# Sliding-window attention and gated FFN on one core: the first w_gate group in halves of x, a hundred small matmuls on zeros, two weight loads in two pieces

## The chip, the core and the metric

The kernel runs on one core of one Trainium2 chip. The core has five engines that run side by side and wait for each other through semaphores: TensorE (PE) does matmuls, with its weight loads shown apart (PEld); VectorE (DVE), ScalarE (ACT) and GpSimd (POOL) work on elements; SyncE (SP) starts transfers. POOL starts most of the loads here. The metric is the device time of one execution in microseconds, the median of several runs. Before the change it is 298.24 us, from 298.19 to 298.33 in three runs.

## What is computed

Attention over 8 batches of 8 heads, 576 positions of depth 64, where each position sees itself and the 63 before it. Its output, laid out as 4608 tokens of 512, goes through a gated feed-forward block.

```python
scores = scale * np.matmul(q, k.transpose(0, 1, 3, 2))
rel = pos[:, None] - pos[None, :]
scores = np.where((rel >= 0) & (rel < 64), scores, -1000000000.0)
attn = softmax(scores)                       # over the last axis
x = np.matmul(attn, v)                       # as [4608, 512]
gate = np.maximum(x @ w_gate, 0.0)           # w_gate, w_val: [512, 1536]
out = gate * (x @ w_val) @ w_out             # w_out: [1536, 512]
```

## The kernel before

**Tokens and tiles.** Attention works in units of 192 positions. The feed-forward block takes tokens in tiles: tile 0 has 384 (units 0 and 1), tile 1 has 192 (unit 2), tile 2 has 448, all later ones 512. From tile 2 on, products are formed by seven instead of eight block products (fast_hidden, L740; SevenOut, L966); tiles 0 and 1 use plain matmuls. The operands are 16 bits wide, the sums 32.

**Weights.** Model depth 512 is cut into four chunks c = 0..3 of 128, the 1536 hidden units into twelve blocks f = 0..11 of 128. w_gate and w_val are each loaded in thirds (f = 0..3, 4..7, 8..11), each third as two loads (w_load, L155 to L163): half a = 0 has c = 0 and 1, half a = 1 has c = 2 and 3. POOL issues them, one after another, among loads of q, k, v and w_out. In the built program each of POOL's loads also waits until the load eight before it has landed. w_out comes in thirds of one load each (L162).

**The start.** q and k of batch 0 are loaded; DVE and ACT turn them into 16 bits (L193) and DVE transposes them (L200). Meanwhile PE writes the mask's bias into all eight banks (bias_mm, L244), and matmuls on zeros (keep_hot, L241; heat, L238) stand at some places between real ones. Scores (L277), exp on ACT (L311), then P·V (u_pv, L348) for units 0 and 1, each in two halves hh of four heads. The norm of a half (reciprocal L362, then multiplication on DVE, L369, or on ACT, L381) and a transpose on DVE (u_turn, L391) give a half of x: half hh = 0 is depth c = 0 and 1, half hh = 1 is c = 2 and 3. P·V of unit 0 lies in banks 0 and 1, that of unit 1 in banks 2 and 3, and the first hidden blocks go to the same four banks, so each bank must have been read by its norm first. The order on DVE is unit 0 half 0, unit 0 half 1, unit 1 half 0, unit 1 half 1.

**first_hidden (L646).** f = 0..3 of tile 0, in four blocks n of 384 columns, each in one bank. Block 0 is f = 0 and 1 on unit 0; block 1 is f = 2 on both units; block 2 is f = 3 on both units; block 3 is f = 0 and 1 on unit 1. A list STEPS says in which order (block, chunks c, units, whether it ends) PE goes through them, first for w_gate (relu on ACT, L677), then for w_val (the product with the relu on DVE, the gate, L683 and L686). Blocks 1 and 2 of w_gate are done in matmuls of 384 columns (L667), all others in matmuls of 192 (L672).

**hidden (L590).** f = 4..11 of tile 0 and all f of tile 1 (L634), relu L605, gate L609. The argument halves = {(first f, 0 for w_gate or 1 for w_val): count} says how many blocks at the front of a group of four are run with c = 0, 1 for all of them before c = 2, 3. SPLIT lists the blocks whose 384 columns are done as two matmuls of 192.

**output (L1168, out_mm L1138).** Tile 0 with the first 128 tokens of tile 1, in four subs of 128 tokens and three cuts of f (0..3, 4..7, 8..11). For OUT_SPLIT <= f < 11 a 512-wide matmul is done as two of 256.

**The order.** One program order is written by hand and by a planner. A Weaver keeps a clock: matmuls advance it by their estimated time, and work of the other engines is put in at a planned time (W.at) or when a landing time given with w_load has come (w_need). So an engine's order follows from estimates, and the chip then runs each engine's queue in that order. Work of unit 2 (its scores, exps, masks L318, P·V and v copies on POOL, L216) is put among the hidden blocks of tile 0 in this way.

Of the kernel before, what the change touches and what calls it, by code (L numbers as in the profile page):

```python
# [10 lines left out]
FP32 = mybir.dt.float32  # L11
FP16 = mybir.dt.float16
# [35 lines left out]
def kernel(  # L48
# [10 lines left out]
    nc = tc.nc  # L59
# [7 lines left out]
    NC = DM // 128  # L67
    NF = DF // 128
    G = 4
    scale = 1.0 / float(D) ** 0.5  # L70
    TT = 2 * U
# [17 lines left out]
    singles = [psum.tile([128, 512], FP32, name=f"bank{i}") for i in range(8)]  # L89
# [9 lines left out]
    us = persist.tile([128, 4, 2, 128 * HF], FP16)  # L99
# [33 lines left out]
    def v_fixed(i, eng):  # L133

        eng.memset(v16s[i][:, :, :, D:VW].bitcast(FP32), ONE_ONE)
        eng.memset(v16s[i][0:64, 0].bitcast(FP32), 0.0)
# [6 lines left out]
    units = {}  # L143
# [3 lines left out]
    def xt_tile(t):  # L147
        if t not in xts:
            xts[t] = x_sb.tile([128, NC, WT], FP16, name="xt")
        return xts[t]  # L150
# [1 line left out]

    w_done = {}

    def w_load(wt, src, f0, f1, landed):  # L155

        if wt is not wo:
            ns = slice(128 * f0, 128 * f1)
            for a in range(2):
                nc.gpsimd.dma_start(wt[:, 2 * a:2 * a + 2, ns], src.rearrange("(a p e) n -> a p e n", a=2, e=2)[a, :, :, ns])  # L160
        if wt is wo:
            nc.gpsimd.dma_start(wo[:, f0:f1], src.rearrange("(c p) n -> p c n", p=128)[:, f0:f1])  # L162
        w_done.update(((wt.name, f, a), landed - 1.3 * (1 - a)) for f in range(f0, f1) for a in range(2))  # L163

    def w_need(wt, f, a=1):
        while (wt.name, f, a) not in w_done:
            W.pop()
        W.advance(w_done[wt.name, f, a])
# [7 lines left out]
    def qk_load(b, name, hh):  # L176

        tile_ = nat[b, name, hh] = nats[:, 2 * "kq".index(name) + hh]
        src = (q if name == "q" else k)[b, G * hh:G * hh + G]
        nc.gpsimd.dma_start(tile_, src.rearrange("h (i j) d -> (h i) (j d)", i=32))  # L180
# [21 lines left out]
    def v_load(u, parts=None):  # L202

        b, uu = divmod(u, UB)
        for g, lo, hi in parts or (((1, 0, 128), (3, 0, 128)), ((5, 0, 128),), ((7, 0, 128), (NG - 1, 64, 128)))[uu]:
            nc.gpsimd.dma_start(v16s[b % 2][lo:hi, g, :, 0:64],  # L206
                                v[b, :, 64 * g - 64 + lo:64 * g - 64 + hi].rearrange("h p d -> p h d"))
# [27 lines left out]
    def heat(n, to, start=True):  # L235

        for _ in range(n):
            nc.tensor.matmul(to, zero[:, 0:128], zero[:, 0:to.shape[1]], start=start, stop=start, skip_group_check=not start)  # L238
# [9 lines left out]
    def one_bank():  # L248
        taken["one"] += 1
        to = singles[(taken["one"] - 1) % 4]  # L250
        while id(to) in unread:
            W.pop()
        return to
# [9 lines left out]
    def st_tiles(u):  # L263
        d = units.setdefault(u, {})
        if u == 0:
            d["st"] = [one_bank() for _ in range(G)]
        else:
            halves = [two_banks() for _ in range(2)]
            d["st"] = halves[0] + halves[1]
        part_written(d["st"])  # L270
        d["p"] = [None] * G
# [23 lines left out]
    def u_st(u, hhs=(0, 1)):  # L295
        d = units.setdefault(u, {})
        if "st" not in d:
            st_tiles(u)
        run_rows([[st_block(d["st"][g][:, U * hh + 64 * w:U * hh + 64 * w + 64], g, hh, UB * u + w, "biased" in d)
                   for hh in hhs for w in range(UB)] for g in range(G)])  # L300
        return 0.29 * len(hhs)
# [117 lines left out]
    def part_written(banks):  # L419
        written.update((id(to), 0) for to in banks)  # L420
# [225 lines left out]
    def first_hidden():  # L646

        g_sb, done = gs[0] = g_sb_p.tile([128, NF, WT], FP16, name="g_sb"), {}
        xt = xt_tile(0)
        r2s = [f_sb.tile([128, 2, WT], FP32, name="pr", bufs=4) for _ in range(2)]  # L650
        r_sbs = [r2s[n // 2][:, n % 2, 0:TT] for n in range(4)]
        blocks = (((0, 0), (1, 0)), ((2, 0), (2, 1)), ((3, 0), (3, 1)), ((0, 1), (1, 1)))
        parts = lambda tile: tile.rearrange("p (w n) -> p w n", w=2)
        STEPS = (
            ((0, (0, 1), (0, 1), False), (0, (2, 3), (0, 1), True), (1, (0, 1), (0, 1), False), (2, (0, 1), (0, 1), False), (1, (2, 3), (0, 1), True), (2, (2, 3), (0, 1), True), (3, (0, 1, 2, 3), (0, 1), True)),
            ((0, (0, 1), (0, 1), False), (2, (0, 1), (0, 1), False), (0, (2, 3), (0, 1), True), (2, (2, 3), (0, 1), True), (3, (0, 1, 2, 3), (0, 1), True), (1, (0, 1, 2, 3), (0, 1), True)),
        )

        def products(h, i, n, cs, us=(0, 1), more=False):
            wt = (wg, wv)[i]  # L660
            block = blocks[n]
            W.advance(W.clock)
            w_need(wt, block[-1][0], cs[-1] // 2)
            whole = i == 0 and n in (1, 2)
            for c in cs if whole else ():
                f = block[0][0]
                nc.tensor.matmul(h[:, 0:TT], wt[:, c, f * 128:f * 128 + 128], xt[:, c, 0:TT],  # L667
                                 start=(c == 0), stop=(c == NC - 1), skip_group_check=True)
            for m in () if whole else us:
                f, u = block[m]  # L670
                for c in cs:
                    nc.tensor.matmul(h[:, U * m:U * m + U], wt[:, c, f * 128:f * 128 + 128], xt[:, c, U * u:U * u + U],  # L672
                                     start=(c == 0 and m == us[0] and not more), stop=(c == NC - 1), skip_group_check=True)
            W.clock += len(us) * len(cs) * (U + 7) / 2400.0

        def relu(n, h):
            nc.scalar.activation(r_sbs[n], h[:, 0:TT], ACT.Relu)  # L677

        def gate(n, h):
            (f, u), (f1, u1) = blocks[n]  # L680
            if f == f1:
                to = g_sb[:, f:f + 1, 0:TT]
                nc.vector.tensor_tensor(to, r_sbs[n].rearrange("p (w n) -> p w n", w=1), h[:, 0:TT].rearrange("p (w n) -> p w n", w=1), MUL)  # L683
                done[f] = TT
            else:
                nc.vector.tensor_tensor(g_sb[:, f:f + 2, U * u:U * u + U], parts(r_sbs[n]), parts(h[:, 0:TT]), MUL)  # L686
                done.update({f: U * u + U, f1: U * u + U})

        for i, then in enumerate((relu, gate)):
            hs = {}  # L690
            for n, cs, us, ends in STEPS[i]:
                more = n in hs
                if not more:
                    hs[n] = one_bank()
                    part_written([hs[n]])
                products(hs[n], i, n, cs, us, more and 0 not in us)
                if ends:
                    W.at(W.clock, lambda n=n, h=hs[n], then=then: then(n, h))
# [186 lines left out]
    wts = persist.tile([128, 4, HF, QN], FP16)  # L885
# [296 lines left out]

    LAST = len(widths) - 1
    BY_ACT = ()
    SPLIT, OUT_SPLIT = [(i, f) for i in range(2) for f in range(4, NF)], 7
    HALVED = [(4, 0, 'P5')] + [(4, 1, name) for name in ('P1', 'P2', 'P3', 'P4')]
    FAST_OUT = (LAST - 5, LAST - 4, LAST - 3, LAST - 2, LAST - 1, LAST)
    O_SUMS = {2: [(24.0, 2, (1, 1)), (26.0, 0, (0, 1))], 3: [(8.0, 3, (1, 0)), (34.0, 1, 2), (34.1, 3, 0)]}
# [8 lines left out]
    with tc.manual_schedule():  # L1197
        G3, V3, O3 = ([(wt, src, f0, f0 + 4) for f0 in (0, 4, 8)]
                      for wt, src in ((wg, moe_w_gate), (wv, moe_w_val), (wo, moe_w_out)))
# [2 lines left out]
            first_load(name)  # L1202
        for name in "kq":
            qk_load(0, name, 1)
        warm = consts.tile([128, 2], FP32)
        nc.vector.memset(warm, 0.0)
        nc.scalar.activation(warm[:, 1:2], warm[:, 0:1], ACT.Exp)
        for i in range(2):
            v_fixed(i, nc.vector)
        zero32 = wts.rearrange("p a f n -> p (a f n)").bitcast(FP32)[:, 0:384]  # L1210
        nc.vector.memset(zero32, 0.0)
        zero = zero32.bitcast(FP16)
        st_tiles(0)
        bands()
        v_load(0, ((1, 0, 128), (3, 0, 64)))
        v_load(1, ((3, 64, 128), (5, 0, 128)))
        w_load(*G3[0], 15.2)
        w_load(*V3[0], 17.7)
        k_zeros()
        band_bias()  # L1220
# [25 lines left out]
        u_turn(0, (0,))  # L1246
        for hh in range(2):
            u_pv(1, (hh,), True)
        heat(1, units[1]["st"][3])
        for hh in range(2):  # L1250
            u_recip(1, (hh,))
        u_norm_act(1, 1)
# [4 lines left out]
        w_load(*G3[1], 20.3)  # L1257
        w_load(*V3[1], 22.8)
        v_load(2)
        w_load(*G3[2], 27.0)  # L1260
        w_load(*V3[2], 29.6)
        W.at(22.0, lambda: u_st(2))
        plan_exps(22.0, 2)
        plan_values(26.4, 2)
# [96 lines left out]

        W.advance(15.3)
        first_hidden()
        hidden(0, ((0, TT),), 4, NF, 4, split=SPLIT, halves={(8, 0): 4, (8, 1): 3})
        hidden(1, ((0, U),), each=4, banks=[0, 1, 4, 5, 2, 3, 0, 1, 2, 3, 0, 1])
        taken["one"] += 2
        output(0, (0, 1, 2, 3), (0, 4, 8, NF))
# [71 lines left out]
```

## Time and profile before

| what | value |
|---|---|
| median of 3 runs | 298.24 us (298.19 to 298.33) |
| the profiled execution | 298.17 us |
| its span, first to last instruction | 296.5 us |
| PE busy | 286.9 us, 97% of the span, 4659 matmuls |
| DVE / ACT / POOL busy | 255.4 / 203.5 / 190.2 us |
| DMA queue of POOL's loads | 49376 packets, 20.26 MB, 57.9% of 16 engines' span |

The profile lists instructions with engine, source line, result and operands. A matmul's duration is its whole passage; how fast matmuls follow each other is read from their starts. "idle before" and "<-" tell how long an engine had nothing to run and what ended that. The chain of work that ended last is followed back from the last instruction, at each step to what released it. The view of transfers gives the time from a load's issue to its landing; issue plus that time is when its data are there.

### The profile page before, as it was taken

The page shows a single profiled execution, that of the slowest core. Times are in us where ns is not written, and L with a number is a line of the kernel's source. Part 1 is how long each engine was busy: PE and PEld are TensorE (multiplying, and loading weights), DVE is VectorE, ACT ScalarE, POOL GpSimd, SP SyncE. Part 2 cuts the span into 40 slices and gives each one's busy share as a digit, 9 for nine tenths or more (in the row PEclk, how much of TensorE's full clock was granted, in tenths as well). Part 3 has the DMA queues.
Part 4 walks back from the last instruction along what each step waited for, and adds up shares of the span by engine and source line. Part 5 has one row for each costly group of instructions (what it writes and reads, how often), then busy time and mean ns, then how long its engine had stood idle before and what let it go on. Part 6 is the DMA issues. An engine that isn't in the chain of part 4 may idle for free.

```text
span 296.5 us, 11064 instructions
## 1 busy us (share of the span) xinstructions
PE 286.9 (97%) x4659; PEld 241.8 (82%) x4659; DVE 255.4 (86%) x513; ACT 203.5 (69%) x409; POOL 190.2 (64%) x217
## 2 busy tenths in 40 slices
PE   4799999999999999999999999999999999999995
PEld 2489966996588657998888888888888888888894
DVE  5988989888889799999999999999858985896585
ACT  3744367888288849983897489857985798538860
POOL 8767667898918628476948594859275617441751
PEclk9999999999999999999999999999999999999999
DMA  7999999987998689911599149913911210021013
GB/s 217 185 197 202 195 194 200 237 102 145 156 211 160 103 140 168 212 51 38 85 219 120 42 69 219 127 48 70 172 24 38 75 38 0 3 95 51 1 39 106
DMA packets 62610, 35.22 MB, mean 119 GB/s; under 512 B 39648, under 2 KB 56672, under 8 KB 62560
## 3 DMA queue, kind: packets, MB, share of 16 engines
q0 software_dynamic: 49376, 20.26, 57.9%
q1 hardware_dynamic: 12752, 13.93, 15.2%
q8 instruction: 36, 0.59, 0.8%
q10 hardware_dynamic: 432, 0.33, 0.3%
q14 instruction: 14, 0.11, 0.1%
HBM read 37.75 MB, written 9.44 MB: 159 GB/s over the span
## 4 chain that ended last, share of the span: by engine, by line
PE 94%; DVE 3%; DMA 1%; ACT 0%; issue 0%; DVEq 0%
PE bank L740 49%; PE bank L966 19%; PE bank L874 7%; PE bank L634 6%; PE bank L277 4%; PE bank L1145 4%; PE bank L493 3%; DMA vs<-in_k_dram 1%; PE bank L672 1%; DVE qT L200 1%; DVE kT L200 1%; PE bank L348 1%; PE bank L667 0%; PE bank L241 0%; ACT nats L193 0%; DVE pr L1133 0%
## 5 line engine op out<-in xcount | busy, mean ns | idle before, releaser
L765 POOL TENSOR_TENSOR g_sb<-pr 128x512 f16<-128x512 f32 (+1 forms) x36 | 46.3, 1288 | 50.0 <-ACT pr L782 46.5
L776 DVE TENSOR_TENSOR pr<-bank,pr 128x512 f32<-128x512 f32 (+1 forms) x96 | 60.8, 673 | 4.1 <-ACT pr L759 2.2
L759 ACT COPY pr<-bank 128x512 f32<-128x512 f32 (+1 forms) x96 | 51.1, 588 | 13.8 <-PE bank L740 13.4
L765 DVE TENSOR_TENSOR g_sb<-r,bank 128x512 f16<-128x512 f32 (+1 forms) x48 | 32.4, 676 | 20.1 <-ACT r L809 18.0
L966 PEld LDWEIGHTS <-g_sb 128*128 128x128 f16 x444 | 41.8, 98 | 5.0
L740 PE MATMUL bank<-xc,us 128*128 128x256 f16 (+2 forms) x292 | 42.7, 269 | 0.0
L740 PE MATMUL bank<-xc,vs 128*128 128x256 f16 (+2 forms) x292 | 42.7, 269 | 0.0
L206 POOL DMA_DIRECT2D v<-in_v_dram x41 | 36.8, 1114 | 6.9 <-DMA nats<-in_q_dram 1.5
L740 PEld LDWEIGHTS <-vs 128*128 128x128 f16 x392 | 37.7, 98 | 3.8
L740 PEld LDWEIGHTS <-us 128*128 128x128 f16 x392 | 37.6, 98 | 3.7
L782 ACT ACTIVATE pr<-pr 128x512 f32<-128x512 f32 (+1 forms) x48 | 30.3, 632 | 8.4 <-DVE pr L776 8.4
L450 ACT ACTIVATE pw<-bank 128x512 f16<-128x512 f32 x60 | 32.0, 606 | 2.0 <-PE bank L277 1.6
L809 ACT ACTIVATE r<-bank 128x512 f32<-128x512 f32 (+1 forms) x48 | 28.8, 600 | 5.1 <-PE bank L740 4.1
L740 PEld LDWEIGHTS <-wg 128*128 128x128 f16 x300 | 28.4, 98 | 3.1
L740 PEld LDWEIGHTS <-wv 128*128 128x128 f16 x300 | 28.4, 98 | 2.7
L740 PE MATMUL bank<-xt,wg 128*128 128x256 f16 (+2 forms) x200 | 28.5, 267 | 0.0
L740 PE MATMUL bank<-xt,wv 128*128 128x256 f16 (+2 forms) x200 | 28.5, 267 | 0.0
L916 POOL TENSOR_TENSOR g_sb<-g_sb,xus 128x512 f16<-128x512 f16 x24 | 27.1, 1147 | 0.0
L966 PE MATMUL bank<-wo,g_sb 128*128 128x256 f16 (+1 forms) x222 | 26.6, 270 | 0.0
L749 ACT COPY bank<-bank 128x512 f32<-128x512 f32 (+1 forms) x48 | 25.6, 576 | 0.0
L966 PE MATMUL bank<-wts,g_sb 128*128 128x256 f16 (+1 forms) x222 | 25.6, 270 | 0.0
L459 DVE TENSOR_TENSOR pw<-pw,mask 128x512 f16<-128x512 f16 x60 | 23.2, 429 | 2.2 <-ACT pw L450 1.7
(125 smaller groups left out, 519.5 us busy)
## 6 DMA issues: line engine op xcount, KB each, us to landing
out_dram<-o_sb SPq DMA_DIRECT2D x31, 256.0 KB, 4.0
nats<-in_k_dram POOLq DMA_DIRECT2D x15, 288.0 KB, 5.9
nats<-in_q_dram POOLq DMA_DIRECT2D x15, 288.0 KB, 7.0
v<-in_v_dram POOLq DMA_DIRECT2D x31, 128.0 KB, 8.6
v<-v SPq DMA_DIRECT2D x12, 132.0 KB, 3.4
v<-v SPq DMA_DIRECT2D x24, 66.0 KB, 2.6
wg<-in_moe_w_gate_dram POOLq DMA_DIRECT2D x6, 256.0 KB, 6.8
wv<-in_moe_w_val_dram POOLq DMA_DIRECT2D x6, 256.0 KB, 8.4
```

Of the source, the lines that this page charges most:

```text
L206: nc.gpsimd.dma_start(v16s[b % 2][lo:hi, g, :, 0:64], v[b, :, 64 * g - 64 + lo:64 * g - 64 + hi].rearrange("h p d -> p h d"))
L450: nc.scalar.activation(d["p"][g].rearrange("p n c -> p (n c)"), d["st"][g], ACT.Exp, scale=scale)
L459: nc.vector.tensor_tensor(d["p"][g], d["p"][g], mask[:, None, :].to_broadcast([128, 2 * QW, 64]), MUL)
L740: nc.tensor.matmul(to[:, HT * m + lo:HT * m + lo + step], w[:, k, 128 * m:128 * m + 128], x[:, k, lo:lo + step], start=(first and m == 0 a ...
L749: nc.scalar.copy(at[j, "B", i][:, 0:TW], at[j, "A", i][:, 0:TW])
L759: nc.scalar.copy(pr[:, i], at[j, "A", i][:, 0:TW])
L765: eng.tensor_tensor(gh[:, f:f + 2, h], pair(r), pair(v), MUL)
L776: nc.vector.tensor_tensor(pr[:, i], to[:, 0:TW], pr[:, i], ADD)
L782: nc.scalar.activation(pr[:, 0], pr[:, 0], ACT.Relu)
L809: nc.scalar.activation(r, to[:, 0:TW], ACT.Relu)
L916: eng.tensor_tensor(to, x, y, op)
L966: nc.tensor.matmul(at[key][:, QN * m * whole:QN * m * whole + n1 - n0], A[:, 128 * m:128 * m + 128], B[:, c, n0:n1] if len(B.shape) == 3 e ...
```

## The change

- w_load gets an argument parts: a half may be loaded in several pieces of columns. w_gate's half a = 0 of the last third comes as two loads of 256 columns (f = 8, 9, then f = 10, 11); so does w_val's half a = 1.
- STEPS is a new list. Blocks 1 and 2 of w_gate are done by units, in matmuls of 192 columns; in the w_gate list a None stands for one heat matmul into bank 7, which stood behind P·V of unit 1 before. In the w_val list, block 3's first two chunks come earlier.
- A hundred matmuls on zeros (128 rows, 32 result rows, 64 columns) into bank 7 stand ahead of the bias, and the memset of the zeros is DVE's first instruction.
- OUT_SPLIT is 2 instead of 7.
- halves: f = 4..7 has the first two blocks by halves for both weights; the last third of w_val two instead of three.

```diff
-    def w_load(wt, src, f0, f1, landed):
+    def w_load(wt, src, f0, f1, landed, parts=(1, 1)):
...
-            ns = slice(128 * f0, 128 * f1)
-            for a in range(2):
+            for a, n, m in ((a, n, parts[a]) for a in range(2) for n in range(parts[a])):
+                ns = slice(128 * f0 + 512 // m * n, 128 * f0 + 512 // m * (n + 1))
...
-            ((0, (0, 1), (0, 1), False), (0, (2, 3), (0, 1), True), (1, (0, 1), (0, 1), False), (2, (0, 1), (0, 1), False), (1, (2, 3), (0, 1), True), (2, (2, 3), (0, 1), True), (3, (0, 1, 2, 3), (0, 1), True)),
-            ((0, (0, 1), (0, 1), False), (2, (0, 1), (0, 1), False), (0, (2, 3), (0, 1), True), (2, (2, 3), (0, 1), True), (3, (0, 1, 2, 3), (0, 1), True), (1, (0, 1, 2, 3), (0, 1), True)),
+            ((0, (0, 1), (0, 1), False), (1, (0, 1), (0,), False), (2, (0, 1), (0,), False), None,
+             (0, (2, 3), (0, 1), True), (1, (2, 3), (0,), False), (2, (2, 3), (0,), False),
+             (1, (0, 1), (1,), False), (2, (0, 1), (1,), False), (3, (0, 1), (0, 1), False),
+             (1, (2, 3), (1,), True), (2, (2, 3), (1,), True), (3, (2, 3), (0, 1), True)),
+            ((0, (0, 1), (0, 1), False), (2, (0, 1), (0, 1), False), (3, (0, 1), (0, 1), False), (0, (2, 3), (0, 1), True), (2, (2, 3), (0, 1), True), (3, (2, 3), (0, 1), True), (1, (0, 1, 2, 3), (0, 1), True)),
...
-            whole = i == 0 and n in (1, 2)
-            for c in cs if whole else ():
-                f = block[0][0]
-                nc.tensor.matmul(h[:, 0:TT], wt[:, c, f * 128:f * 128 + 128], xt[:, c, 0:TT],
-                                 start=(c == 0), stop=(c == NC - 1), skip_group_check=True)
-            for m in () if whole else us:
+            for m in us:
...
-            for n, cs, us, ends in STEPS[i]:
+            for step in STEPS[i]:
+                if step is None:
+                    heat(1, singles[7])
+                    continue
+                n, cs, us, ends = step
...
-    SPLIT, OUT_SPLIT = [(i, f) for i in range(2) for f in range(4, NF)], 7
+    SPLIT, OUT_SPLIT = [(i, f) for i in range(2) for f in range(4, NF)], 2
...
+        zero32 = wts.rearrange("p a f n -> p (a f n)").bitcast(FP32)[:, 0:384]
+        nc.vector.memset(zero32, 0.0)
+        zero = zero32.bitcast(FP16)
+        for i in range(100):
+            nc.tensor.matmul(singles[7][32 * (i % 4):32 * (i % 4) + 32, 0:64], zero[:, 0:32], zero[:, 0:64], start=True, stop=True, skip_group_check=True)
...
-        zero32 = wts.rearrange("p a f n -> p (a f n)").bitcast(FP32)[:, 0:384]
-        nc.vector.memset(zero32, 0.0)
-        zero = zero32.bitcast(FP16)
...
-        heat(1, units[1]["st"][3])
...
-        w_load(*G3[2], 27.0)
-        w_load(*V3[2], 29.6)
+        w_load(*G3[2], 27.0, (2, 1))
+        w_load(*V3[2], 29.6, (1, 2))
...
-        hidden(0, ((0, TT),), 4, NF, 4, split=SPLIT, halves={(8, 0): 4, (8, 1): 3})
+        hidden(0, ((0, TT),), 4, NF, 4, split=SPLIT, halves={(4, 0): 2, (4, 1): 2, (8, 0): 4, (8, 1): 2})
```

In the built program this moves two things that the diff does not name: DVE's fourth mask of unit 2 (L318) comes ahead of the first gate of f = 4..7 (L609) instead of behind it, and four matmuls of w_gate's f = 8 come ahead of unit 2's P·V on PE. Behind these, the order on every engine is the one from before, but for the finer matmuls of the output.

## The prediction

> **What bounds the kernel now.** I read the page first: TensorE (PE) is busy for 97% of the span, and the chain that ended last is nearly all PE.
>
> ```profile
> PE 94%; DVE 3%; DMA 1%; ACT 0%; issue 0%; DVEq 0%
> ```
>
> So only what shortens or lengthens PE's row of matmuls counts, or the few us ahead of it. The chain in order of time shows where that row begins.
>
> ```profile
> 13.59 0.20 DVE r L362
> ...
> 14.06 0.43 DVE xus L369
> 14.49 0.49 DVE xt L391
> 14.99 0.04 issue
> 15.03 0.49 PE bank L672 x4
> 15.52 1.45 PE bank L667 x8
> 16.97 3.30 PE bank L672 x40
> 20.27 1.98 PE bank L634 x24
> ```
>
> From 15.03 to 291.70 the chain is PE alone. Before 15.03 it runs through VectorE (DVE), which makes x. PE's timeline shows the place in detail (start, duration, then the operation).
>
> ```profile
> 4.42 2.72 PE L244 MATMUL bank<-bias,ident 128*128 128x384 f16 x8 [4.42 <-DVE bias L130]
> 6.93 1.43 PE L241 MATMUL bank<-wts 128*128 128x384 f32 x2
> 8.35 0.55 PE L277 MATMUL bank<-qT,kT 32*128 32x64 f16 x48
> 9.13 0.91 PE L241 MATMUL bank<-wts 128*128 128x384 f32 x2 [0.23 <-ACT p L311]
> ...
> 13.57 0.39 PE L238 MATMUL bank<-wts 128*128 128x512 f16 x1
> 13.80 0.49 PE L672 MATMUL bank<-xt,wg 128*128 128x192 f16 x4
> 15.03 0.49 PE L672 MATMUL bank<-xt,wg 128*128 128x192 f16 x4 [0.74 <-DVE xt L391]
> 15.49 1.47 PE L667 MATMUL bank<-xt,wg 128*128 128x384 f16 x8
> 16.80 0.82 PE L672 MATMUL bank<-xt,wg 128*128 128x192 f16 x8
> 17.46 2.80 PE L672 MATMUL bank<-xt,wv 128*128 128x192 f16 x32
> ```
>
> Two things are to be seen. PE has nothing to run from 14.29 to 15.03, waiting for the second half (depth c = 2, 3) of unit 0 of x; and L667's first matmul waits again, since four 192-wide ones from 15.03 would have ended at 15.36. Early on, matmuls are slow: eight of 384 columns start within 2.51 us (4.42 to 6.93), 314 ns apart, while L667's 384-wide ones take (16.80-15.49)/8 = 164 ns. The granted-clock row shows full speed all along, so the slow start shows in these spacings only.
>
> **The change, part by part.** Times are on the profiled execution: span 296.5 us, execution 298.17 us, 0.07 under the median of 298.24.
>
> 1. *The w_gate group.* Removed: the 384-wide matmuls; the same work is 192-wide, and each four for a unit's half come as soon as that half is there. Spacing of 192-wide: (17.46-16.80)/8 = 82.5 ns, so 2 x 82.5 = 165 against 164; nothing lost. Ahead of 15.03 there are now four more: two into bank 1, free when ScalarE's (ACT) last L381 for it ends at 14.05, and two into bank 2, free when DVE L369 ends at 13.98+0.52 = 14.50. They end at about 14.72. The moved 512-wide heat (0.216 us, spacing below) then ends at 14.93, 0.10 ahead of x. From 15.03, 24 matmuls of 82.5 ns remain: 1.98 us, to 17.01 instead of 17.46. Their inputs arrive in time: unit 1's first half by 15.48 (needed after 8, 15.69), its second by 16.05 (needed after 16, 16.35), bank 3 free at 15.44 (needed 16.02). Term: **-0.45 us**.
>
> 2. *The w_val group follows 0.45 earlier.* It needs w_val's second half landed by 17.01+12x0.0825 = 18.00; issue 9.48 plus about 8.0 gives 17.5. Its third block needs the second relu gone from bank 2 at 17.67; relus in a row start 0.39 apart (16.68, 17.07) and take 0.49, so it ends near 17.6. No stall, with 0.05 to spare. The second thirds: w_gate's second half lands at 12.95+7.1 = 20.05; with the new halves it is needed after eight matmuls, 19.65+0.66 = 20.31. w_val's lands at 14.34+8.7 = 23.05, needed at 22.88+0.66 = 23.54. Bound: 0 to 0.1 each. I take 0.
>
> 3. *Around unit 2 the gain is partly given back.* The built order differs here: the fourth mask (L318) stands on DVE ahead of the first gate (L609), and four w_gate matmuls into that gate's bank stand ahead of unit 2's P·V (L348).
>
> ```profile
> 24.65 0.54 DVE L609 TENSOR_TENSOR g_sb<-pr,bank 128x384 f16<-128x384 f32 x1
> 25.12 0.72 DVE L318 TENSOR_TENSOR p<-p,mask 128x384 f16<-128x384 f16 x1
> ```
>
> ```profile
> 23.75 1.88 POOL L216 COPY v<-v 64x512 f16<-64x512 f16 x2 [2.69 <-DMA v<-in_v_dram]
> ```
>
> The mask waits for the fourth exp, which ends at 24.28+0.52-0.45 = 24.35; it holds DVE for 0.65 (25.12 to the next at 25.76), the gate takes 0.54: 24.43+0.65+0.54 = 25.62, plus the signal 25.66, against 25.52 when PE comes: 0.14 us late. The P·V behind it needs GpSimd's (POOL) copies L216. In the program each POOL load waits for the load eight before it; with two more loads the last piece waits for the one that lands at 23.05, is issued near 23.3, and the copies start at 24.05, end at 25.93. P·V comes at about 26.08 after the 0.14; without it, at 25.94 it would wait for them anyway. Term: **+0.14** (0 to 0.3).
>
> 4. *The two loads in pieces.* POOL issues two loads more of 0.71 us, hidden in its 0.42, 0.53, 0.58 and 2.69 us waits, but for the 0.3 in step 3. Landings: 256 KB loads land 1.26 us apart; a 128 KB load of v, with rows of 128 bytes, lands about 0.65 after the one before it, so a 128 KB piece with longer rows costs 0.63 to 0.70, and both pairs together at most 0.15 over the whole loads. Behind them w_out's first third lands at 29.46+10.2 = 39.66, needed at 40.49-0.31 = 40.18; its second at 32.27+11.6 = 43.87, needed near 44.3. Term: 0 (0 to 0.2). If the cover goes, PE waits at L1145 for the difference.
>
> 5. *Output of tile 0 in 256-wide matmuls for f = 2..10 instead of 7..10.* Five more f for four subs: 20 matmuls of 512 become 40 of 256. In windows narrow enough for single instructions, L1145's 512-wide start 216 ns apart, its 256-wide 109.2: 2 x 109.2-216 = 2.4 ns each. Term: **+0.05**.
>
> 6. *A hundred small matmuls and the earlier memset.* DVE's memset of the zeros (0.38) goes ahead of 1.1 us of others; DVE is idle until the mask at 4.18, so nothing waits. PE is idle until 4.42. No row shows these matmuls; nearest is L348 with the same 128*32 tile and 65 columns: 48 start in 0.36 us (26.07 to 26.43), 7.5 ns each, doubled for the slow start 15 ns: 1.5 us, from 1.3 to 2.8. Upper bound, one after another at the slow rate: 64/384 x 314 = 52 ns, to 6.5, with the bias matmuls behind them. I take the first, as its tile is the same: term 0. If the early work brings the fast rate forward, bias and keep_hot end near 6.8 rather than 8.35, but the scores wait for DVE's qT (7.04+1.26 = 8.30) all the same: 0 again.
>
> Sum: -0.45+0.14+0.05 = -0.26 us; 298.17-0.26 = 297.91. **Forecast 297.9 us.** Later orders on all engines are the same as before, and PE has no wait there, so the shift is carried to the end.
>
> **The rivals.** *A, nothing given back:* the exp or the mask is quicker (a mask without POOL beside it takes 0.36, the first at 23.31) and P·V stays 0.4 ahead: 298.17-0.40 = 297.77, or down to 297.5 if splitting has a gain that no row shows. Against it: step 3 has two separate locks, DVE and POOL.
>
> *B, another transfer takes the wait's place:* w_gate's second half at 20.05 against 20.31 and w_out's at 43.87 against 44.3 are the near ones; 0.25 us of DMA delay eats the rest: 298.2. The saving then shows as a PE wait on a DMA.
>
> *C, the change does not do what it says:* if DVE's L369 ends 0.1 us later, the heat stands in front of the matmuls at 15.03 and costs up to its 0.22: 298.1.
>
> *D, slower: PE's rate falls back.* If the small matmuls raise the rate early, PE then runs out at 6.8 and idles until 8.35, which before it never did. A row for an idle stretch that lowers the rate does not exist in this trace: gaps of 0.74 (14.29) and about 0.5 us (10.0 to 10.51) left it fast. If 1.5 us of idling is the point from which it decides, all between 10.51 and 13.6 runs at half rate: first scores +0.4, P·V +0.4, keep_hot +0.5 (1.43 against 0.91), P·V +0.4 less what overlaps, about +1.4 on the chain: 298.17-0.26+1.4 = 299.3. The Trainium skill, "TensorE: Matmul & The Clock Gate", Part 1, speaks to this: PE runs at half clock until an activity window of about 3.4 us has been busy, the window is free-running, and an idle window takes it back. By that page 1.5 us is less than a window, so the fall would not come unless a mostly idle window counts as idle; the trace agrees that half rate ends some 3.4 to 3.9 us after 4.42, and shows no fall.
>
> *E, slower: the small matmuls run one by one* (step 6's upper bound): scores start near 9.3 instead of 8.35 and ACT's exps push the rest by 0.9: 298.8.
>
> **How the numbers follow.** Forecast 0.57 (297.65 to 298.1); A 0.14, of which half below 297.64; B and C 0.15 (298.0 to 298.5); D 0.08; E 0.06. The range 297.5 to 298.7 leaves out most of D and E and little of A. Against the median, 0.2% is 0.60 us, about what a measurement tells from no change: faster below 297.64, slower above 298.84. Faster 0.13 (half of A and an edge of the forecast), same 0.74, slower 0.13.
>
> **What would show it.** Right: w_val's first matmul near 17.01; no idle PE from 14.3 to 14.9 but for a short wait at bank 2; a PE wait of about 0.1 us near 25.5 to 26 for DVE's gate or POOL's copy; first output matmul near 40.2. Step 6: small matmuls over by 3, L241 starting before 6.93. Wrong: L277 at 10.5 or L348 at 11.3 starting 15 ns apart or more; a wait for a DMA at L634 or L1145; a heat that ends behind 15.03.

## The result and the profile after

The changed kernel takes 299.65 us (median of six runs, 299.35 to 300.15); the kernel before took 298.30 beside it (six runs, 298.19 to 298.98). The ratio is 1.0044, with an interval from 1.0033 to 1.0055: slower, where 297.9 and a range up to 298.7 had been forecast. The profiled execution took 299.37 us against 298.17, so 1.20 us more are to be found. First the page of the changed kernel: span, PE's row, the queue that brings instructions, the chain's shares.

```profile
span 297.7 us, 11322 instructions
...
PE 289.0 (97%) x4787; PEld 245.7 (83%) x4787; DVE 255.6 (86%) x513; ACT 203.1 (68%) x409; POOL 191.8 (64%) x219
...
q8 instruction: 37, 0.61, 0.8%
...
PE 93%; DVE 3%; DMA 1%; ACT 1%; issue 0%; DVEq 0%
```

PE runs 128 matmuls more (4787 against 4659) and is 2.1 us longer busy, and q8 has one packet more (before: 36). The line of q8 looks like nothing and turns out to be the main clue to the experiments. PE's timeline of the changed kernel answers to the one shown of before:

```profile
1.40 1.52 PE L1211 MATMUL bank<-wts 128*32 128x64 f16 x100 [1.40 <-DVE warm L1213]
4.41 2.72 PE L244 MATMUL bank<-bias,ident 128*128 128x384 f16 x8 [1.48 <-DVE bias L130]
6.92 1.48 PE L241 MATMUL bank<-wts 128*128 128x384 f32 x2
9.22 0.55 PE L277 MATMUL bank<-qT,kT 32*128 32x64 f16 x48 [0.82 <-DVE qT L200]
...
11.38 0.55 PE L277 MATMUL bank<-qT,kT 32*128 32x64 f16 x48 [0.46 <-DVE qT L200]
...
14.45 1.30 PE L670 MATMUL bank<-xt,wg 128*128 128x192 f16 x8
15.59 0.38 PE L238 MATMUL bank<-wts 128*128 128x512 f16 x1
15.91 2.14 PE L670 MATMUL bank<-xt,wg 128*128 128x192 f16 x24
17.88 0.82 PE L670 MATMUL bank<-xt,wv 128*128 128x192 f16 x8
```

The small matmuls run as forecast, from 1.40 to 2.7 us. But the first scores come at 9.22 instead of 8.35, and everything is late from there. By places:

| place | before | after | difference |
|---|---|---|---|
| k's first load has landed | 4.65 | 5.21 | +0.56 |
| first scores | 8.35 | 9.22 | +0.87 |
| x's second half, PE goes on | 15.03 | 15.91 | +0.88 |
| w_val's first matmul | 17.46 | 17.88 | +0.42 |
| tile 0's first output matmul | 40.49 | 41.29 | +0.80 |
| tile 2's first matmul | 52.70 | 53.85 | +1.16 |
| last matmul | 292.79 | 293.98 | +1.19 |

So: 0.88 lost before x, 0.46 gained in the w_gate group, 0.38 lost around unit 2, and 0.36 lost in the output of tile 0. Of the first, DVE's rows show where it comes from:

```profile
5.23 0.46 DVE L193 CAST nats<-vs 128x576 f16<-128x576 f32 x1 [0.88 <-DMA vs<-in_k_dram]
5.93 1.26 DVE L200 STREAM_TRANSPOSE kT<-nats 128x576 f32<-128x576 f32 x1 [0.24 <-ACT nats L193]
7.04 0.77 DVE L193 CAST nats<-vs 128x576 f16<-128x576 f32 x1
```

The same casts before:

```profile
4.68 0.60 DVE L193 CAST nats<-vs 128x576 f16<-128x576 f32 x1 [0.31 <-DMA vs<-in_k_dram]
6.49 0.45 DVE L193 CAST nats<-vs 128x576 f16<-128x576 f32 x1
```

The k cast waits 0.56 longer for its load, and the q cast takes 0.77 us (0.45 before). It now starts in the middle of POOL's last issue of v (L206, 6.62 to 7.52) and ends 0.28 us behind that issue's end, as it does in the five other kernels below in which it takes 0.77 to 0.78; in two where k came later still and the cast started at 7.20 and 7.21, near the issue's end, it took 0.44 to 0.45. That the issue holds it up is inferred from these times. The loss in the output is one interval of 0.42 us between two L1147 that should start 0.11 apart, at 52.77 us, and nothing in the profile is named for it.

### The profile page after: what moved, and what is told of

The parts are those of the page before. It is cut to its first block, busy times and chain, and to the rows that moved or that the text cites. A ratio compares the mean times of both kernels' runs of the same rounds, so it can differ in the third digit from the quotient of the medians.

```text
span 297.7 us, 11322 instructions
## 1 busy us (share of the span) xinstructions
PE 289.0 (97%) x4787; PEld 245.7 (83%) x4787; DVE 255.6 (86%) x513; ACT 203.1 (68%) x409; POOL 191.8 (64%) x219
## 4 chain that ended last, share of the span: by engine, by line
PE 93%; DVE 3%; DMA 1%; ACT 1%; issue 0%; DVEq 0%
PE bank L742 49%; PE bank L968 19%; PE bank L876 7%; PE bank L634 5%; PE bank L1147 4%; PE bank L277 4%; PE bank L493 3%; PE bank L670 2%; DMA vs<-in_k_dram 1%; DVE qT L200 1%; DVE kT L200 1%; PE bank L348 1%; ACT p L311 1%; DVE p L318 0%; PE bank L241 0%
## 5 line engine op out<-in xcount | busy, mean ns | idle before, releaser
L206 POOL DMA_DIRECT2D v<-in_v_dram x41 | 36.9, 1119 | 6.0 <-issue 2.4
```

The lines of the kernel that those rows point to most:

```text
L206: nc.gpsimd.dma_start(v16s[b % 2][lo:hi, g, :, 0:64], v[b, :, 64 * g - 64 + lo:64 * g - 64 + hi].rearrange("h p d -> p h d"))
```

## The experiments

Sizes of standstills are the time between two matmuls' starts less the first one's own time (taken as columns/2.4 ns; 512 columns start 216 ns apart). "The 449th" and the like count PE's rows in the trace from 0: weight loads, matmuls and eight others. A matmul is two rows, its weight load and itself.

**First, parts alone.** The small matmuls alone (the memset's three lines leave their old place), all but them, OUT_SPLIT alone, and the new order with neither:

```diff
+        zero32 = wts.rearrange("p a f n -> p (a f n)").bitcast(FP32)[:, 0:384]
+        nc.vector.memset(zero32, 0.0)
+        zero = zero32.bitcast(FP16)
+        for i in range(100):
+            nc.tensor.matmul(singles[7][32 * (i % 4):32 * (i % 4) + 32, 0:64], zero[:, 0:32], zero[:, 0:64], start=True, stop=True, skip_group_check=True)
         warm = consts.tile([128, 2], FP32)
```

> The kernel before with one part alone: the memset of the zeros first on DVE and the hundred small matmuls behind it. In the profile of the changed kernel the first load of k lands at 5.21 instead of 4.65 us and the second scores start at 11.38 instead of 10.51. Theory S (the small matmuls, or the memset ahead of them, delay the start): about 298.3 + 0.87 = 299.2 us, with the second scores near 11.4. Rival N (the late landing was chance, one execution against another): 298.3, second scores near 10.5.

The second is the changed kernel with the memset in its old place and without

```diff
-        for i in range(100):
-            nc.tensor.matmul(singles[7][32 * (i % 4):32 * (i % 4) + 32, 0:64], zero[:, 0:32], zero[:, 0:64], start=True, stop=True, skip_group_check=True)
```

> The changed kernel without the hundred small matmuls and with the memset of the zeros in its old place. Theory S: 299.65 - 0.87 = 298.8 us. Rival N: 299.65, no change. Under both the four w_gate matmuls of f = 8 wait near 26 us for DVE's gate (0.38 us there), and a wait of 0.3 us near the end of tile 0's output stays if it comes from the finer output.

The third is the kernel before with

```diff
-    SPLIT, OUT_SPLIT = [(i, f) for i in range(2) for f in range(4, NF)], 7
+    SPLIT, OUT_SPLIT = [(i, f) for i in range(2) for f in range(4, NF)], 2
```

> The kernel before with OUT_SPLIT 2 alone. By the spacing of matmuls: +0.05 us, 298.35. Rival I: the forty more instructions drain PE's instruction buffer, and PE stands for 0.3 us near the end of the output until the next refill is there: 298.65, with an idle stretch that ends by issue.

The fourth is the second with this line as before:

```diff
-    SPLIT, OUT_SPLIT = [(i, f) for i in range(2) for f in range(4, NF)], 2
+    SPLIT, OUT_SPLIT = [(i, f) for i in range(2) for f in range(4, NF)], 7
```

> The changed kernel without the small matmuls (memset in its old place) and with OUT_SPLIT 7: what is left is the new order of the first group with its heat, the halves and the two loads in pieces. Theory: -0.46 for the filled gap and +0.38 for the wait at the gate: 298.2. Rival N: the late start belongs to this part (its loads or its order): 299.1 or more. Were the wait at the gate gone without the late start: 297.9.

Measured: small matmuls alone 300.89 us (ratio 1.0083, 1.0055 to 1.0111); all but them 303.16 (1.0177, 1.0144 to 1.0209); OUT_SPLIT alone 301.59 (1.0111, 1.0086 to 1.0137); the order alone 299.28 (1.0042, 1.0025 to 1.0059). Each of the four is slower, three by more than the whole change, so the parts do not add, and no expectation had a term for what came. That the small matmuls bring the late start is borne out: k lands at 5.04 with them alone, and at 4.64 to 4.76 in the three without them. Forty instructions more in tile 0's output cost 3.2 us, the greater part of it 60 us behind the place where they stand. The chain of OUT_SPLIT alone, in order of time:

```profile
112.68 0.61 PE bank L277 x58
113.29 1.95 issue
115.23 0.21 PE bank L277
115.44 0.97 PE bank L874 x2
```

"issue" is time in which PE waits for nothing that the profile names, here in the middle of 64 score matmuls. Counting PE's rows up to each such place gave the theory: they are the 449th, 1729th, 1985th, 3777th or 7873rd row, and all these are 193 more than a multiple of 256. The packets of q8 have 16384 bytes, there is one for each 256 of PE's rows (9326 rows and 36 packets before, 9582 and 37 after), and one had started 2.2 to 2.4 us ahead of the end of each of these standstills.

**The refill theory:** PE's instructions come in blocks of 256; a border is the first row of a block. The first packet is taken to be that of the block at the 449th row, the second that of the 705th, and so on. The packet for the next block starts at some time around the first instruction of a block (from 1.8 us ahead of it to 4.4 us behind it), and the next block's first instruction can't run until 2.2 to 2.6 us after that start. A block that PE gets through sooner ends in a standstill. What decides is where the borders lie, so an instruction added anywhere moves every later border: no step of the prediction had a term for that. The rival is that the added work brings its standstills with it.

**Tests of it.** The kernel before with the early memset alone; with 128 small matmuls, which are one whole block; OUT_SPLIT 2 with 108 of them (40 + 216 = 256); and the new order with OUT_SPLIT 7 and 120 behind the old memset (16 + 240 = 256). The second and the third differ from the kernel with a hundred by

```diff
-        for i in range(100):
+        for i in range(128):
```

(108 in the third, with OUT_SPLIT 2), and the fourth has

```diff
         zero = zero32.bitcast(FP16)
+        for i in range(120):
+            nc.tensor.matmul(singles[7][32 * (i % 4):32 * (i % 4) + 32, 0:64], zero[:, 0:32], zero[:, 0:64], start=True, stop=True, skip_group_check=True)
         st_tiles(0)
```

> The kernel before with the memset of the zeros ahead of the other memsets, and no small matmuls. Both kernels with the hundred small matmuls had k's first load land at 5.21 and 5.04 us instead of 4.65, VectorE's second cast at 0.770 us instead of 0.445, and PE at x's second half 0.88 and 0.71 us late. If the earlier memset does this: landing at about 5.1, second cast 0.77, time about 299.0 us. If the small matmuls do it: landing at 4.65 (to 4.77, the most of the kernels without them), second cast 0.445, time that of the kernel before, 298.3 us within 0.3.

> The kernel before with the early memset and 128 small matmuls, 256 PE instructions. Refill theory (every 256th PE instruction, the 193rd, 449th and so on of the trace, runs no sooner than about 2.2 us after a packet of 16384 bytes for PE has started, and PE stands still where the schedule would have it sooner): 256 instructions more shift every later instruction by one whole block, so each block holds what it held before, and no stall named issue over 0.4 us is left, the 1.12 us at 231 us of the kernel with 100 included; what stays is the early delay of 0.7 to 0.9 us: about 299.1 us (298.9 to 299.5). Rival (each small matmul costs, or the stalls come with more instructions whatever their number): with 28 more of them at least the 300.9 us of the kernel with 100.

> The kernel with OUT_SPLIT 2 alone (301.6 us, stalls of 1.09 us at 50.8 and 2.01 us at 115.2) with the early memset and 108 small matmuls added: 40 and 216 are 256 PE instructions. Refill theory: the two stalls go (under 0.4 us each, since the 40 do not all lie ahead of 50 us), the early delay of 0.7 to 0.9 us comes: about 299.2 us (298.9 to 299.7), faster by 2.4 us for more work. Rival (the divided outputs cost the stalls themselves): the stalls stay and the early delay comes on top, 302.3 us.

> The changed kernel with OUT_SPLIT 7, with the memset in its old place and 120 small matmuls behind it (from about 2.5 us instead of 1.4): 16 instructions of the new order and 240 are 256. Refill theory: no stall at 17.0, 50.9 or 115.8 us. If the early delay came from the early memset or from the small matmuls in the first 2.5 us: k lands at 4.65, x's second half is taken at 15.03, w_val's first matmul at 17.01, and with the 0.2 to 0.4 us that the gate's wait at 26 us gives back the time is about 298.1 us (297.9 to 298.3). If small matmuls beside k's load delay it wherever they stand: 0.7 to 0.9 us more, 298.9 us.

The memset alone: 298.39 us, ratio 0.9998 (0.9989 to 1.0007), k at 4.72: it is not the memset. Its profiled execution is the slowest of ten, 299.17 us, with 0.71 us at the 449th row, where the packet had started 0.8 us later than in the kernel before. OUT_SPLIT 2 with 108 small matmuls: 299.81 (1.0063, 1.0042 to 1.0084), just above the 298.9 to 299.7 expected, and faster than without them by 1.8 us, for 216 instructions more; the rival, 302.3, falls. The standstill at 115 us is gone, as its timeline shows, all 64 scores in one run:

```profile
112.50 0.68 PE L277 MATMUL bank<-qT,kT 32*128 32x64 f16 x64
113.12 2.77 PE L874 MATMUL bank<-wo,g_sb 128*128 128x512 f16 x12
115.82 0.69 PE L277 MATMUL bank<-qT,kT 32*128 32x64 f16 x64
116.43 0.61 PE L740 MATMUL bank<-xt,wg 128*128 128x256 f16 x4
```

The one near 51 us shrank from 1.10 to 0.60 (1985th row, 53.12 us), more than the 0.4 expected. With 128, and with 120 behind the memset, no border has a standstill over 0.2 us, as expected; the times (301.37 from 299.09 to 302.37; 299.60 from 299.25 to 302.52) missed, though the lowest with 128 is at the 299.1 expected. Their profiled executions are the slowest of each and lost time to two other things. The first is PE's clock at the start. With 128, the record of full speed begins at 13.76 us (8.53 in the changed kernel), and L241, 0.91 us at full speed, takes 1.65 at 10.04. With 120 behind the memset, full speed comes early, at 5.99, PE then waits 1.73 us, and the clock is at half again from 12.82 to 16.23:

```profile
6.47 0.81 PE L241 MATMUL bank<-wts 128*128 128x384 f32 x2
9.00 0.55 PE L277 MATMUL bank<-qT,kT 32*128 32x64 f16 x48 [1.73 <-DVE qT L200]
...
13.43 1.65 PE L241 MATMUL bank<-wts 128*128 128x384 f32 x2
```

x's second half is taken at 16.48 and 17.15 in these two, against 15.91 in the changed kernel. The second is one of DVE's sums, in both at the same place. DVE's rows of the kernel with 128:

```profile
47.34 0.42 DVE L561 TENSOR_TENSOR us<-us,wg 128x512 f16<-128x512 f16 x1
47.80 3.63 DVE L561 TENSOR_TENSOR us<-wg,us 128x512 f16<-128x512 f16 x1
51.36 1.37 DVE L561 TENSOR_TENSOR us<-wg 128x512 f16<-128x512 f16 x1
```

and POOL's:

```profile
47.78 1.15 POOL L561 TENSOR_TENSOR vs<-wv,vs 128x512 f16<-128x512 f16 x1
48.90 1.14 POOL L561 TENSOR_TENSOR vs<-wv 128x512 f16<-128x512 f16 x1
50.01 1.14 POOL L561 TENSOR_TENSOR us<-wg 128x512 f16<-128x512 f16 x1
51.23 1.22 POOL L561 TENSOR_TENSOR us<-us,wg 128x512 f16<-128x512 f16 x1
```

DVE's third sum starts 0.02 us behind POOL's first and lasts until three of POOL's are over: 3.63 us instead of 0.42, and tile 2 starts at 55.8, behind a PE wait of 1.50 us. DVE comes there with PE, POOL with its transfers. In the kernel before, DVE's fourth sum ends 0.80 us ahead of POOL's first start (47.22 and 48.02), in the changed kernel 0.01 us ahead (48.36 and 48.37): a little more delay, and it would be over this edge too. In both of these kernels k came late again (5.13 and 4.98 us), so the small matmuls do that also where they start at 2.5 us.

**A prediction against the grain, and the other two steps.** The kernel before with the early memset and 60 small matmuls; the changed kernel with the old halves; and that with OUT_SPLIT 7 and 120 small matmuls:

```diff
-        for i in range(100):
+        for i in range(60):
...
-        hidden(0, ((0, TT),), 4, NF, 4, split=SPLIT, halves={(4, 0): 2, (4, 1): 2, (8, 0): 4, (8, 1): 2})
+        hidden(0, ((0, TT),), 4, NF, 4, split=SPLIT, halves={(8, 0): 4, (8, 1): 3})
```

> The kernel before with the early memset and 60 small matmuls, 120 PE instructions. In all five kernels with 100 to 128 of them one of the 16 shares of k's first load landed 0.45 to 0.69 us behind the other 15 (before: 0.05), and of q's too. With 60, the 193rd PE instruction is no longer a small matmul at 2.6 us but one of the first scores at about 8.5 us. If the request for PE's next 16384 bytes holds up one share: all 16 within 0.1 us of the next, k at 4.65 to 4.77, VectorE's second cast 0.445 us. If the small matmuls themselves hold it up: one share some 0.3 us late, k at about 4.95. Refill theory on where PE stands still, before it runs: the boundaries lie 120 instructions earlier in the work than in the kernel before, so one block has only 4.6 us (from 8.5 to 13.1) and one 2.2 us (74.3 to 76.6): with refills that start up to 3.7 us after the block before began and are of use 2.2 to 2.4 us later, a stall of about 1 us at the 449th instruction (the values' matmuls, L348, near 13.2 us) and one of 1 to 3 us at the 2753rd (L493, near 77 us); about 301 us. Rival (stalls at places of their own, whatever the count): none at those two instructions.

> The changed kernel with the old halves of the units from 4 on, {(8, 0): 4, (8, 1): 3}, so that VectorE's gate of f = 4 stands ahead of the fourth mask again; everything else as changed. If the place of the gate is what the 0.38 us at 26.8 us come from: the wait goes, output and tile 2 come 0.3 to 0.4 us earlier than 41.29 and 53.85, about 299.3 us instead of 299.65. If the gap's gain pushes PE into the gates whatever their order: the wait stays and the time with it, 299.6 us.

> The changed kernel with the old halves, OUT_SPLIT 7 and 120 small matmuls instead of 100: its instructions ahead of every later place are 256 more than in the kernel before (16 and 240), one block. If three things make the whole difference (the gap's gain of 0.46 us, the early delay of 0.75 to 0.9 us that stays here, and the stall and the gate's wait that go), the time is 298.3 - 0.46 + 0.8 = about 298.6 us (298.5 to 298.9). If something else is in it: 299.0 us or more.

Sixty took 309.09 us (ratio 1.0329, 1.0296 to 1.0363), 8 us more than a hundred. Both standstills are where they had been put, at the 449th row and at the 2753rd (a weight load; its matmul is the next row). In PE's timeline of this kernel:

```profile
13.98 0.24 PE L348 MATMUL bank<-v,p 128*32 128x65 f16 x5
15.49 0.51 PE L348 MATMUL bank<-v,p 128*32 128x65 f16 x43 [1.28 <-issue]
...
81.07 1.27 PE L493 MATMUL bank<-v,pw 128*32 128x65 f16 x124
84.22 0.21 PE L493 MATMUL bank<-v,pw 128*32 128x65 f16 x4 [1.89 <-issue]
```

Three more of 0.9 to 1.7 us, which I had not worked out, came at the 1729th, 3777th and 4033rd, 4.2 us together. The time is 8 us above the 301 expected; the rest is the late k (first scores at 9.23 instead of 8.35), about 0.7 us at half clock behind the first standstill, over 1 us of waits in tile 2's first matmuls, near 57 to 64 us, and two small standstills at the 7105th and 8129th. k was late with 60 too (5.21 us), so it is not the request for PE's next block that delays it: that theory fell.

With the old halves the wait for the gate went, but not the time: 299.88 us (1.0041, 1.0026 to 1.0055). The gate now stands ahead of the fourth mask, that mask ends at 26.63, and P·V waits 0.28 us for it instead; and the standstill at the 1985th row grew from 0.31 to 0.86. With OUT_SPLIT 7 and 120 small matmuls on top: 299.29 us (1.0034, 1.0018 to 1.0049), above the 298.6 to 298.9 expected. Its timeline shows what was forgotten in that sum:

```profile
15.82 1.48 PE L670 MATMUL bank<-xt,wg 128*128 128x192 f16 x16
17.64 0.82 PE L670 MATMUL bank<-xt,wg 128*128 128x192 f16 x8 [0.34 <-DVE us L561]
```

The first of the eight is the 705th row; its packet started at 15.15, 2.49 us earlier. DVE is named because its event came last, but PE stood 0.50 us for the packet. With borders as in the kernel before, one lies in the w_gate group, at the 449th row, which there ran at 16.80 us, 2.55 us behind the start of its packet at 14.25. That lies within the 2.2 to 2.6 at which standstills end: closing the gap ahead of it runs into the refill. That is also the 1.24 us at 17.03 in the kernel with the order alone.

**The smallest edit.** The kernel before with the early memset and eight small matmuls, 0.06 us of PE:

```diff
-        for i in range(100):
+        for i in range(8):
```

> The kernel before with the early memset and 8 small matmuls, done by 1.6 us, ahead of the first packet of k's load at 1.83 us. One of k's 16 shares landed 0.45 to 0.71 us behind the others in all eight kernels with 60 to 128 small matmuls, whatever their number. If it is the matmuls' running beside the load, none is late here: k at 4.65 to 4.77 us. If it is enough that PE has begun, or if the program laid out for these kernels does it, one is late by about 0.5 us again: k at about 5.2. Refill theory: the boundaries lie 16 instructions earlier in the work than in the kernel before; the block that ends near 15.5 us has 4.8 us and the one that ends near 50.6 us 4.5 us instead of 6.0 and 5.4, so with a refill some 3.6 and 2 us after the block before and 2.3 us more, a stall of about 1 us at the 449th instruction (in w_gate's first group, near 16.5 us) and a short one, under 0.6 us, at the 1729th (near 51 us): 299.0 to 300.5 us. Rival (stalls grow with the small matmuls): 298.4 us.

299.17 us (ratio 1.0053, 1.0020 to 1.0085), k on time at 4.72, and the standstill at the 449th row:

```profile
15.10 0.49 PE L672 MATMUL bank<-xt,wg 128*128 128x192 f16 x4 [0.74 <-DVE xt L391]
16.49 1.46 PE L667 MATMUL bank<-xt,wg 128*128 128x384 f16 x8 [0.91 <-DVE us L561]
```

In the kernel before, the second of these lines starts at 15.49. Eight matmuls that nothing waits for, ended at 1.6 us, cost 0.8 us at 16: all seven executions take 299.16 us or more, while of the ten with the memset alone nine take 298.20 to 298.59. The 1729th row has no standstill to be seen, within the "under 0.6".

All runs by the number of PE's rows added:

| kernel | rows added | median us | standstills at borders, us (row) |
|---|---|---|---|
| before; early memset | 0 | 298.3; 298.39 | none; 0.71 (449) in its profile |
| 8 small; order alone | 16 | 299.17; 299.28 | 1.07 (449); 1.24 (449) |
| OUT_SPLIT 2 alone | 40 | 301.59 | 1.10 (1729), 2.11 (3777) |
| all but the small | 56 | 303.16 | 0.81 (449), 1.87 (1729), 1.78 (3777) |
| 60 small | 120 | 309.09 | 1.45 (449), 0.91, 2.05, 1.63, 1.69 (1729 to 4033), 0.36 (7105), 0.23 (8129) |
| 100 small alone | 200 | 300.89 | 1.12 (7873) |
| the change | 256 | 299.65 | 0.31 (1985) |
| OUT_SPLIT 2, 108 small | 256 | 299.81 | 0.60 (1985) |
| 128; 120 behind | 256 | 301.37; 299.60 | none; none |
| change with old halves | 256 | 299.88 | 0.86 (1985), 0.30 (4033) |
| that, 120 small, OUT_SPLIT 7 | 256 | 299.29 | 0.50 (705) |

In the 14 profiles 498 blocks begin behind a recorded packet, and none began less than 2.19 us after its packet's start. None of these kernels beats the kernel before.

## Why the prediction was wrong, step by step

The forecast was -0.26 us, and the profiled execution shows +1.20. Three terms make up the 1.46 between: the small matmuls (step 6, put at nothing) cost 0.88 at the start; the mask beside POOL's copy (step 3) cost 0.24 more than its 0.14; and a refill in the output (step 5), which no step had, cost 0.31. That is 1.43.

1. **The w_gate group, -0.45: right.** w_val's first matmul is 0.456 us nearer to x. That it stays in the changed kernel is owed to the 200 rows of the small matmuls, which move the border out of this group (the 705th row runs at 18.87, 3.06 us behind its packet). Without them it is eaten there.
2. **The w_val group, 0: right.** No wait appears; PE's starts run through.
3. **Around unit 2, +0.14 (0 to 0.3): too small, 0.38.** The gate behind the fourth mask is the wait, as said. Mis-sized was the mask. It starts right behind its exp, at 25.26 (as worked out, but for the 0.88 of the late start), but holds DVE for 0.93 us and not 0.65, because it now lies beside POOL's second copy (L216, 24.99 to 26.05) until that is over; 0.14 + 0.28 is 0.42. In the kernel before and in the two with the old halves, too, DVE's next operation starts 0.13 to 0.14 us behind the end of that copy. DVE's rows in the changed kernel, the four masks and the gates behind them:

```profile
23.73 2.53 DVE L318 TENSOR_TENSOR p<-p,mask 128x384 f16<-128x384 f16 x4 [0.71 <-ACT p L311]
26.18 1.94 DVE L609 TENSOR_TENSOR g_sb<-pr,bank 128x384 f16<-128x384 f32 x4
```

   The old halves showed that the order of gate and mask is not the remedy: whichever comes second is late, by 0.38 or 0.28.
4. **The loads in pieces, 0: right** as far as seen; no PE wait for a load appears at L634 or L1147.
5. **OUT_SPLIT, +0.05: the price of the matmuls was right, the step failed.** In the changed kernel the row of outputs is longer by 0.36, of which 0.31 is the standstill at the 1985th row. Alone, the edit costs 3.2 us, by standstills at 51 and 115 us.
6. **The small matmuls, 0: failed, the largest miss.** They run in 1.3 us, hidden, as said, and do not bring the fast rate forward (full speed is on record from 8.53 us, 8.18 before). But "nothing waits for them" overlooked two things: k's load lands 0.56 later beside them, and DVE's q cast, pushed later, takes 0.32 more; together the 0.88 that outweighs the gain. And their 200 rows move all borders, which no step priced.

The rivals: A, B and C did not occur. D and E were the slower ones, with 299.3 and 298.8 near the outcome. That nearness is chance, since neither is what the changed kernel's profile shows: the small matmuls are not one by one, and the clock's record is at full speed from 8.53 us to the end. D's course (full speed early, idle, half clock) is on record in one profiled execution, of the kernel with 120 small matmuls behind the memset; so it can happen with small matmuls, though not in the execution that is explained here.

What stays open. Why k's load is late beside 60 or more small matmuls: of the 16 shares in which the profile sees it land, the last came 0.44 to 0.71 us behind the one before it in all eight such kernels, and no more than 0.11 in the six others. In the eight, one packet of the load that started at 2.12 to 2.17 us took 0.89 to 1.63 us; in the six others no packet of it took over 0.86. It is not the memset, not their number from 60 on, not their place (from 1.4 or from 2.5 us), not the request for the next block. With 120 behind the memset the long packet started at 2.15, ahead of the first small matmul at 2.48, and ended at 3.17. And what sets the start of a packet, which came from 1.8 us ahead of to 4.4 us behind the first instruction of the block before it; the late ones lie where loads keep the transfer engines busy, which is a coincidence in time and was not tested.

## What to carry to other kernels

Before pricing an edit that adds or removes PE instructions, count PE's rows: find the borders in the trace (every 256th row), and look whether a run of short matmuls gets through a block in less than about 6.6 us behind a border (a packet that starts 4.4 us late, and 2.2 us more). A standstill named "issue", or put down to an engine that had long been done, at such a row is most likely a refill; and an edit's worth is then read with a number of added rows that leaves the borders where they were. A tuned kernel may be tuned to its borders, so a part tried alone can be far worse than the whole.

## What the runs showed of the hardware

**Instruction refills cost time.** Packets of 16384 bytes took 0.88 to 2.0 us, and no block began sooner than 2.19 us behind one's start; up to 2.1 us were lost at one border. The Trainium skill, "Runtime: NRT & Kernel Launch", section "Instruction fetch mechanics", says that a 16 KiB boundary is mostly hidden. In the kernel before this holds, with 36 packets and no standstill; in the kernel with 60 small matmuls the five largest standstills make 7.7 us.

**The clock can fall behind a short idle time.** In OUT_SPLIT alone the granted clock is at half from 115.23 to 118.64 us, right behind 2.1 us without a matmul, and 512-column matmuls start 426 ns apart instead of 216; with 60 small matmuls it is at half from 15.97 to 19.39, 0.5 us behind the end of a standstill of 1.45 us; with 120 behind the memset, from 12.82 to 16.23, where the longest wait ahead was 1.73 us. It need not fall: standstills of 1.87 us (all but the small) and 2.05 us (60 small) left it at full speed, and what decides is open. The Trainium skill, "TensorE: Matmul & The Clock Gate", Part 1, gives a window of about 3.4 us: the three stretches of 3.41 to 3.42 us agree, but the idle times ahead of them are shorter than a window.
